# Sparse attention and routed experts on one core: a strided mask moved from TensorE to VectorE, one expert's weights loaded three steps later, and two warm-up products fewer

## The chip, the core and the metric

The kernel runs on one core of a Trainium2 chip. A core has five engines that each work through their own list of instructions in order and wait for one another through semaphores: TensorE (PE in the profile; its weight loads are PEld), VectorE (DVE), ScalarE (ACT), GpSimd (POOL) and SyncE (SP), which here issues most of the transfers. The transfers themselves are carried out by 16 DMA engines. The metric is the device time of one execution in microseconds.

## The reference

Eight batches of 576 tokens go through attention with 8 heads of 64, and then through a layer of eight experts of which each token uses one.

```python
# q, k, v: (B=8, H=8, S=576, D=64); stride = 32; scale = 1/8
rel = pos[:, None] - pos[None, :]
mask_local   = (rel >= 0) & (rel < 32)
mask_strided = (rel >= 0) & (pos[None, :] % 32 == pos[:, None] % 32)
# heads 0..3 use mask_local, heads 4..7 mask_strided
attn = softmax(where(mask, scale * q @ k.T, -1e9)) @ v
x = attn.transpose(0, 2, 1, 3).reshape(B, S, 512)
logits = x @ w_gate                       # 8 experts
local_gate = sigmoid(x @ w_local)
for b, s in all tokens:
    fresh = argmax(logits[b, s])
    e = fresh if s == 0 or local_gate[b, s] < 0.5 else previous e
    out[b, s] = softmax(logits[b, s])[e] * (relu(x[b, s] @ w1[e]) @ w2[e])   # w1[e] 512x1024, w2[e] 1024x512
```

A token of a strided head sees only the tokens of its own residue class modulo 32, and of those the ones up to itself.

## The kernel before

**Steps.** The attention stage is one Python loop (L450) over 32 steps, with three more at its end. Step n handles one batch and one pair of heads, n = 4 × batch + pair. Pairs 0 and 1 of a batch are local heads, pairs 2 and 3 are strided heads. Each step has two units (L428), and a unit handles about half the tokens of both heads in one PSUM tile `sps`, of which there are two.

**Local units.** The tokens are cut into spans of 96 queries with the 128 keys that they can see. TensorE multiplies keys by queries (L264), ScalarE takes the exponential (L268), and VectorE multiplies it by a mask of ones and zeros, `maskL` (L275).

**Strided units.** The host has sorted the tokens by residue class. Seven classes of 18 tokens make a block of 126, and the last block has four classes, 72 tokens; a unit has two blocks, or two and the one of 72. Within a block only pairs of the same class in causal order count. Before it adds the scores, TensorE writes the mask into PSUM: an identity matrix times `maskS` (L258), which holds 0 for pairs that count and a value of −8e9 for the others. The scores are added to that (L264, which does not start a new sum there), and the exponential gives zero where the mask is. VectorE has no mask to apply then. The four such mask products of a step are 252 or 324 columns wide. `maskS` is built at the start of the kernel (L209 to L225) from `apart`.

**Order within a step.** A step issues, in this order: the loads of step n + 4 (L451, function `load`: a tile qk of queries and keys, L169, and once per batch and kind the values, vl or vs, L173); a piece of the weights of expert 0 (L454); the scores and masks of its two units; the store of a finished batch half to device memory (`store_x`, L314 and L320, when the pair of step n − 2 is odd); the transposes `turn_x` of step n − 2 (L330); the products with the values (L288) and the normalisation on VectorE (L301, L302) of step n − 1. After these come the gate's logits and the router's work, which `also` spreads over the steps from 19 on. Each engine keeps the order in which its instructions are issued.

**Queues.** All loads of the attention stage and the pieces of the weights are issued by SP, and so are the stores of batches 1 to 7; the stores of batch 0 are issued by POOL. The store of local heads is two transfers, that of strided heads ten. SP's transfers share eight completion semaphores in turn, so that an issue waits for the transfer that was issued eight before it. There are five qk tiles, so that the load of step n + 4 waits until the scores of step n − 1 are done.

**Expert 0.** The weights of the first expert (4 MB) are loaded in eight pieces of 512 KB, one a step, at steps 5 to 12 (L454, L455; transfers at L724 and L727). From step 10 on VectorE takes sums of these pieces (`moe.W[0].sums`, L456, L732; 128x512 operations), two a step at the end of a step (L483). They are needed by the expert stage only, which begins at about 158 us and runs to the end.

**Warm-up.** While the first loads are on their way, TensorE multiplies a tile of zeros ten times (`busy(WARM)`, L186, 128x512 products into `vps`).

Of the kernel before, what the change touches and what calls it, by code (L numbers as in the profile page):

```python
# [8 lines left out]
F32 = mybir.dt.float32  # L9
# [3 lines left out]
Alu = mybir.AluOpType  # L13
# [6 lines left out]
B, H, S, DH = 8, 8, 576, 64  # L20
# [19 lines left out]
GK, GL = PL * GC, PL * GR  # L40
# [15 lines left out]

TRUST = 1e12

WARM = 10

FILL = 4

TWINS = {b: b - 1 for b in range(1, B - 1, 2) if b % RB}

# [20 lines left out]
def across(ap, shape):  # L85

    return ap.rearrange("a (o b) -> a o b", o=1).to_broadcast(shape)
# [60 lines left out]
def attention(ctx, tc, qkl, qks, vl, vs, wg, xd, ident, router, moe):  # L148

    nc = tc.nc  # L150
    sums, probs, codes = router.sums, router.probs, router.codes
    consts = ctx.enter_context(tc.tile_pool(name="consts", bufs=1))
# [11 lines left out]
    def load(b, pair):  # L164
        local = pair < PAIRS // 2
        src = qkl if local else qks
        t = inp.tile([P, qkl.shape[-1]], F32, name="qk")
        st["qk", b, pair] = t
        nc.sync.dma_start(out=t[:, 0:src.shape[-1]], in_=src[b, pair % 2])  # L169
        if pair % 2 == (b == 0 and local):  # L170
            shape = [LK, LT, 4, V1] if local else [GK, GT, 4, V1]
            t = vals.tile(shape, F32, name="vl" if local else "vs")
            nc.sync.dma_start(out=t, in_=(vl if local else vs)[b])  # L173
            st["v", b, local] = t
# [6 lines left out]
    def busy(n):  # L181
        for _ in range(n):
            ps = psV.tile([P, 512], F32, name="vps")
            nc.tensor.matmul(ps, lhsT=warm[:, 0:P], rhs=warm, start=True, stop=True)  # L184

    busy(WARM)  # L186

# [21 lines left out]
    maskS = consts.tile([GK, 2 * GK + GL], BF16, name="maskS")  # L209
# [3 lines left out]
    for n, c in blocks:  # L213

        i, div = consts.tile([GK, 1], I32, name=f"row{n}"), consts.tile([GK, 1], F32, name=f"div{n}")
# [7 lines left out]
    n = GK  # L223
    nc.vector.tensor_copy(maskS[:, 0:2 * n].rearrange("p (a x) -> p a x", a=2), across(apart[n], [n, 2, n]))
    nc.vector.tensor_copy(maskS[:, 2 * n:], apart[GL])  # L225
    fold = consts.tile([P, 32], F32, name="fold")
    ci = consts.tile([P, E], I32, name="ci")
    down = consts.tile([P, E], F32, name="down")
    pi = consts.tile([P, CH], I32, name="pi")
    pos8 = consts.tile([P, CH], F32, name="pos8")  # L230
    start = consts.tile([P, CH], F32, name="start")

    def more_constants():

        nc.vector.tensor_reduce(fold, ident.rearrange("p (k x) -> p x k", k=DK), axis=AX.X, op=Alu.add)


        nc.gpsimd.iota(ci, pattern=[[-1, E]], base=E, channel_multiplier=0)
        nc.vector.tensor_copy(down, ci)
        nc.gpsimd.iota(pi, pattern=[[E * P, CH]], base=E, channel_multiplier=E)  # L240
        nc.vector.tensor_copy(pos8, pi)
        nc.vector.tensor_scalar(start, pos8, float(E), None, Alu.is_equal)

    def spans(u):

        if u.local:
            return [(3 * u.g + i, LQ, i * LQ) for i in range(3)]
        return [(j, GK if j < GT - 1 else GL, i * GK) for i, j in enumerate(range(2 * u.g, 2 + 3 * u.g))]

    def scores(u):  # L250
        t = st["qk", u.b, u.pair]
        kb, width = (LK, LQ) if u.local else (GK, GK)
        ps = psS.tile([P, 2, 512], F32, name="sps")
        sp = spans(u)
        n = sp[-1][2] + sp[-1][1]
        if not u.local:
            for h in range(2):
                nc.tensor.matmul(ps[0:GK, h, 0:n], lhsT=identb[0:GK, 0:GK],  # L258
                                 rhs=maskS[:, 0:n], start=True, stop=False, skip_group_check=True)
        for j, w, c in sp:  # L260
            m = kb if u.local else w
            for h in range(2):
                r = slice(h * DH, (h + 1) * DH)
                nc.tensor.matmul(ps[0:m, h, c:c + w], lhsT=t[r, S + j * width:S + j * width + m],  # L264
                                 rhs=t[r, j * width:j * width + w],
                                 start=(u.local and c == 0), stop=True, skip_group_check=True)
        e = work.tile([P, 2, 2 * GK + GL], F32, name="e")
        nc.scalar.activation(e[0:kb, :, 0:n], ps[0:kb, :, 0:n], Act.Exp, bias=0.0, scale=1.0 / DH ** 0.5)  # L268
        u.e = e

    def mask(u):
        if u.local:
            ev = u.e[:, :, 0:3 * LQ]
            m = maskL[:, 3 * u.g:3 * u.g + 3].rearrange("p a x -> p (a x)")
            nc.vector.tensor_tensor(ev, ev, m.rearrange("p (o x) -> p o x", o=1).to_broadcast([LK, 2, 3 * LQ]),  # L275
                                    op=Alu.mult)

    def values(u):
# [151 lines left out]
        u.n = n  # L430

    also = {n: [] for n in range(len(units) + 3)}
    also[1] = [more_constants]
    also[2] = [router.constants]
    n = PAIRS * RB + 3
# [4 lines left out]
    m = n  # L440
    rooms = (moe.spot[0].rearrange("p a x -> p (a x)")[:, 0:1024], moe.spot[1].rearrange("p a k x -> p (a k x)"),
             moe.spot[2].rearrange("p i a x -> p (i a x)"))
    early = router.table(0, bank, rooms)
# [6 lines left out]
    for n in range(len(units) + 3):  # L450
        if n < len(units):  # L451
            if n + ahead < len(order):
                load(*order[n + ahead])
            if 5 <= n < 13:  # L454
                moe.W[0].load(nc, moe.w1, moe.w2, 0, n - 5)  # L455
            if n == 10:  # L456
                steps = moe.W[0].sums(nc.vector)
            for u in units[n]:
                scores(u)
                mask(u)  # L460
        if 0 <= n - 2 < len(units) and order[n - 2][1] % 2 == 1:
            store_x(units[n - 2][1])
        if 0 <= n - 2 < len(units) and n != len(units):
            turn_x(*order[n - 2])
        if 0 <= n - 1 < len(units):
            for u in units[n - 1]:
                values(u)
                norm(u)
        if n == len(units):
            turn_x(*order[n - 2])  # L470
            moe.turn(moe.first, spare, 0)
        elif n == len(units) + 1:
            busy(FILL)
        for b in range(B):
            last = PAIRS * b + PAIRS - 1
            if n == last + 3 and b + 1 not in TWINS:
                gates(b)
            if n == last + 4 and b < B - 1 and b + 1 not in TWINS:
                for both in {TWINS.get(b, b), b}:
                    store_p(both)  # L480
            if n == last + 2:
                logits(b)
        for do in steps[:2]:  # L483
            do()
            steps.remove(do)
        if n == len(units) + 1:
            moe.turn(moe.first, bank, 1)
            busy(2)
            moe.row_sums(moe.first)
        for do in also[n]:  # L490
            do()
# [1056 lines left out]
```

## Time and profile before

| What | Value |
| --- | --- |
| Time, median of 3 runs | 677.26 us (677.22 to 678.85) |
| Profiled execution: its own time | 677.25 us |
| Profiled execution: span of the core | 675.5 us |
| TensorE busy | 661.2 us, 98% of the span |
| VectorE busy | 353.9 us, 52% |
| ScalarE busy | 195.4 us, 29% |
| Attention stage | about 0 to 158 us |
| Expert stage | about 158 us to the end |

The profile is of one execution. Its span goes from the first to the last instruction, and the execution took 1.75 us more than that. A row of groups or of the timeline names the line, the engine, the operation, the tile written and the tiles read, the shapes, and how often it ran. A bracket with an arrow names what the engine waited for just before. "SPq" is SP issuing a transfer. A line with "DMA" in a chain of waits is the time in which a transfer was under way and somebody waited for it. "PE sps L264" is TensorE at the score products, "PE vps L184" at the products of zeros.

### The profile page before, as it was taken

The page shows a single profiled execution, that of the slowest core. Times are in us where ns is not written, and L with a number is a line of the kernel's source. Part 1 is how long each engine was busy: PE and PEld are TensorE (multiplying, and loading weights), DVE is VectorE, ACT ScalarE, POOL GpSimd, SP SyncE. Part 2 cuts the span into 40 slices and gives each one's busy share as a digit, 9 for nine tenths or more (in the row PEclk, how much of TensorE's full clock was granted, in tenths as well). Part 3 has the DMA queues.
Part 4 walks back from the last instruction along what each step waited for, and adds up shares of the span by engine and source line. Part 5 has one row for each costly group of instructions (what it writes and reads, how often), then busy time and mean ns, then how long its engine had stood idle before and what let it go on. Part 6 is the DMA issues. An engine that isn't in the chain of part 4 may idle for free.

```text
span 675.5 us, 14755 instructions
## 1 busy us (share of the span) xinstructions
PE 661.2 (98%) x6019; PEld 569.9 (84%) x6020; DVE 353.9 (52%) x783; ACT 195.4 (29%) x364; POOL 109.3 (16%) x132
## 2 busy tenths in 40 slices
PE   9999999999999999999999999999999999999995
PEld 6888888888999999599979999996799899699594
DVE  5658876956884447126523664651256546522122
ACT  3545445453312221321222222121222132221320
POOL 3401010122022023012011202302011112121001
PEclk9999999999999999999999999999999999999999
DMA  9998787875311081171145217101712622011001
GB/s 324 391 353 276 267 282 258 280 239 195 124 65 49 18 312 58 28 283 49 36 155 172 65 52 265 64 21 40 262 41 65 220 93 73 34 43 58 17 9 37
DMA packets 36435, 95.85 MB, mean 142 GB/s; under 512 B 4594, under 2 KB 12658, under 8 KB 36262
## 3 DMA queue, kind: packets, MB, share of 16 engines
q1 hardware_dynamic: 28438, 72.59, 30.7%
q0 software_dynamic: 7296, 21.19, 9.8%
q8 instruction: 67, 1.10, 0.7%
q14 instruction: 106, 0.87, 0.4%
q10 hardware_dynamic: 528, 0.10, 0.1%
HBM read 74.69 MB, written 19.69 MB: 140 GB/s over the span
## 4 chain that ended last, share of the span: by engine, by line
PE 94%; DVE 2%; DMA 1%; issue 1%; ACT 0%; SPq 0%; POOL 0%; DVEq 0%; POOLq 0%; ACTq 0%
PE lps L835 30%; PE mps L871 29%; PE sps L264 6%; PE vps L288 6%; PE lps L926 4%; PE mps L937 4%; PE tps L330 3%; PE xps L778 2%; PE mps L967 2%; PE lps L947 2%; PE sps L258 2%; DMA qk<-in_qks_dram 1%; PE tps L354 1%; PE vps L184 1%; PE tps L382 1%
## 5 line engine op out<-in xcount | busy, mean ns | idle before, releaser
L791 POOL DMA_INDIRECT out_dram<-y,tab x40 | 45.8, 1146 | 351.0 <-DVE y L823 246.6
L835 PE MATMUL lps<-tt,ws 128*128 128x128 f32 x768 | 91.5, 275 | 0.0
L835 PEld LDWEIGHTS lps<-tt,ws 128*128 128x128 f32 x768 | 88.5, 192 | 0.2
L871 PE MATMUL mps<-wt,k 128*128 128x256 f32 x384 | 85.7, 380 | 0.0
L871 PEld LDWEIGHTS mps<-wt,k 128*128 128x128 f32 x384 | 72.8, 190 | 9.9
L835 PE MATMUL lps<-xt,w1t 128*128 128x128 f32 x512 | 63.1, 276 | 3.0 <-ACT y L973 1.9
L835 PEld LDWEIGHTS lps<-xt,w1t 128*128 128x128 f32 x512 | 60.4, 192 | 6.5 <-ACT y L973 3.7
L823 DVE TENSOR_TENSOR h<-lps,u 128x512 f32<-128x512 f32 x48 | 33.2, 691 | 58.6 <-PE lps L835 58.5
L871 PE MATMUL mps<-w2t,h 128*128 128x256 f32 x256 | 60.5, 379 | 0.0
L268 ACT ACTIVATE e<-sps 128x576 f32<-128x576 f32 (+1 forms) x64 | 41.7, 651 | 54.7 <-PE sps L264 53.5
L765 POOL DMA_INDIRECT x<-xd,gi x40 | 40.2, 1005 | 82.4 <-PE lps L835 24.0
L871 PEld LDWEIGHTS mps<-w2t,h 128*128 128x128 f32 x256 | 47.4, 190 | 5.8
L264 PE MATMUL sps<-qk 64*128 64x96 f32 (+2 forms) x704 | 50.9, 282 | 0.8 <-DMA qk<-in_qks_dram 0.8
L822 ACT ACTIVATE h<-h 128x512 f32<-128x512 f32 x48 | 30.2, 630 | 70.1 <-DVE h L823 69.0
L264 PEld LDWEIGHTS sps<-qk 64*128 64x128 f32 (+2 forms) x704 | 42.9, 185 | 9.0 <-issue 6.5
L822 ACT ACTIVATE h<-lps 128x512 f32<-128x512 f32 (+1 forms) x28 | 15.6, 563 | 81.8 <-PE lps L835 62.6
L823 DVE TENSOR_TENSOR u<-lps,p 128x512 f32<-128x512 f32 x16 | 11.1, 691 | 51.8 <-PE lps L835 31.4
L771 ACT ACTIVATE x<-x 128x512 f32<-128x512 f32 (+1 forms) x40 | 27.1, 717 | 32.7 <-DMA x<-xd,gi 21.3
L779 ACT COPY xt<-xps 128x512 f32<-128x512 f32 (+1 forms) x38 | 20.3, 565 | 51.4 <-PE xps L778 51.4
L835 PE MATMUL lps<-xt,ws 128*128 128x128 f32 x256 | 31.3, 275 | 0.0
L835 PE MATMUL lps<-tt,w1t 128*128 128x128 f32 x256 | 31.3, 275 | 0.0
L871 PE MATMUL mps<-w2t,k 128*128 128x256 f32 x128 | 30.4, 380 | 0.0
(238 smaller groups left out, 952.2 us busy)
## 6 DMA issues: line engine op xcount, KB each, us to landing
w1t<-in_w_dram SPq DMA_DIRECT2D x7, 2048.0 KB
w2t<-in_w_dram SPq DMA_DIRECT2D x7, 2048.0 KB
qk<-in_qkl_dram SPq DMA_DIRECT2D x16, 592.0 KB
qk<-in_qks_dram SPq DMA_DIRECT2D x16, 576.0 KB
vl<-in_vf_dram SPq DMA_DIRECT2D x8, 780.0 KB
vs<-in_vg_dram SPq DMA_DIRECT2D x8, 639.8 KB
xd<-xl SPq DMA_DIRECT2D x14, 288.0 KB
xd<-xs SPq DMA_DIRECT2D x56, 63.0 KB
```

Source lines behind the costliest of these rows:

```text
L264: nc.tensor.matmul(ps[0:m, h, c:c + w], lhsT=t[r, S + j * width:S + j * width + m], rhs=t[r, j * width:j * width + w], start=(u.local and ...
L268: nc.scalar.activation(e[0:kb, :, 0:n], ps[0:kb, :, 0:n], Act.Exp, bias=0.0, scale=1.0 / DH ** 0.5)
L288: nc.tensor.matmul(ps[a * HALF:(a + 1) * HALF, h, i], lhsT=u.e[0:m, h, q0:q0 + HALF], rhs=vt[0:m, j, 2 * i2 + h], start=(i == 0 and h == 0 ...
L765: self.nc.gpsimd.indirect_dma_start(out=r.x[0:r.m, i], out_offset=None, in_=self.xd[0:r.rows], in_offset=bass.IndirectOffsetOnAxis(ap=r.gi ...
L771: self.nc.scalar.activation(r.x[0:r.m, i, 0:D], r.x[0:r.m, i, 0:D], Act.Copy, scale=r.gate[i][0:r.m])
L791: s = self.nc.gpsimd.indirect_dma_start(out=self.out, out_offset=bass.IndirectOffsetOnAxis(ap=r.si[i][0:r.m], axis=0), in_=y[0:r.m, i], in ...
L822: relu = lambda o, i: nc.scalar.activation(o, i, Act.Relu)
L823: add = lambda o, i, p: nc.vector.tensor_tensor(o, p, i, op=Alu.add)
L835: nc.tensor.matmul(ps[:, f], lhsT=m[:, kk, f * P:(f + 1) * P], rhs=v[:, kk], start=(start and f == 0 and kk == 0), stop=(kk == 1), skip_gr ...
L871: nc.tensor.matmul(ps[:, 0:256], lhsT=m[:, f], rhs=v[:, f], start=(start and f == 0), stop=(f == 3), skip_group_check=True)
L926: nc.tensor.matmul(ps[:, f], lhsT=w.w1[:, kk, c:c + P], rhs=r.xt[:, 0, kk], start=(f == 0 and kk == 0), stop=(kk == DK - 1), skip_group_ch ...
L937: nc.tensor.matmul(ps, lhsT=h[f // 4][:, f % 4], rhs=w.w2[:, f], start=(f == 0), stop=(f == FK - 1))
```

## The change

For the strided pairs of batches 0 and 1 (`MB = 2`) the mask is no longer written into PSUM by TensorE. VectorE multiplies the exponential by `near`, which is 1 where `maskS` is 0 and 0 elsewhere, as it does for local heads. `near` is computed once, at the end of step 0. In the block of 72 such a unit now computes all 126 rows of scores, and the mask sets what is too much to zero. To have rows enough there, queries and keys of strided heads change places in the tile that is loaded, on the host and in the kernel (`k0`, `q0`). Batches 2 to 7 keep the mask on TensorE.

The eight pieces of expert 0's weights are loaded at steps 8 to 15 instead of 5 to 12, and the sums begin at step 13 instead of 10. The warm-up has eight products instead of ten.

```diff
@@ -56,9 +56,11 @@
 
 TRUST = 1e12
 
-WARM = 10
+WARM = 8
 
 FILL = 4
+
+MB = 2
 
 TWINS = {b: b - 1 for b in range(1, B - 1, 2) if b % RB}
 
@@ -223,6 +225,7 @@
     n = GK
     nc.vector.tensor_copy(maskS[:, 0:2 * n].rearrange("p (a x) -> p a x", a=2), across(apart[n], [n, 2, n]))
     nc.vector.tensor_copy(maskS[:, 2 * n:], apart[GL])
+    near = consts.tile([GK, 2 * GK + GL], F32, name="near")
     fold = consts.tile([P, 32], F32, name="fold")
     ci = consts.tile([P, E], I32, name="ci")
     down = consts.tile([P, E], F32, name="down")
@@ -230,6 +233,9 @@
     pos8 = consts.tile([P, CH], F32, name="pos8")
     start = consts.tile([P, CH], F32, name="start")
 
+    def masks():
+        nc.vector.tensor_scalar(near, maskS, 0.0, None, Alu.is_equal)
+
     def more_constants():
 
         nc.vector.tensor_reduce(fold, ident.rearrange("p (k x) -> p x k", k=DK), axis=AX.X, op=Alu.add)
@@ -253,17 +259,20 @@
         ps = psS.tile([P, 2, 512], F32, name="sps")
         sp = spans(u)
         n = sp[-1][2] + sp[-1][1]
-        if not u.local:
+        early = u.b < MB
+        if not u.local and not early:
             for h in range(2):
                 nc.tensor.matmul(ps[0:GK, h, 0:n], lhsT=identb[0:GK, 0:GK],
                                  rhs=maskS[:, 0:n], start=True, stop=False, skip_group_check=True)
         for j, w, c in sp:
-            m = kb if u.local else w
+            m = kb if u.local or early else w
             for h in range(2):
                 r = slice(h * DH, (h + 1) * DH)
-                nc.tensor.matmul(ps[0:m, h, c:c + w], lhsT=t[r, S + j * width:S + j * width + m],
-                                 rhs=t[r, j * width:j * width + w],
-                                 start=(u.local and c == 0), stop=True, skip_group_check=True)
+                k0, q0 = (S, 0) if u.local else (0, S)
+
+                nc.tensor.matmul(ps[0:m, h, c:c + w], lhsT=t[r, k0 + j * width:k0 + j * width + m],
+                                 rhs=t[r, q0 + j * width:q0 + j * width + w],
+                                 start=((u.local or early) and c == 0), stop=True, skip_group_check=True)
         e = work.tile([P, 2, 2 * GK + GL], F32, name="e")
         nc.scalar.activation(e[0:kb, :, 0:n], ps[0:kb, :, 0:n], Act.Exp, bias=0.0, scale=1.0 / DH ** 0.5)
         u.e = e
@@ -273,6 +282,11 @@
             ev = u.e[:, :, 0:3 * LQ]
             m = maskL[:, 3 * u.g:3 * u.g + 3].rearrange("p a x -> p (a x)")
             nc.vector.tensor_tensor(ev, ev, m.rearrange("p (o x) -> p o x", o=1).to_broadcast([LK, 2, 3 * LQ]),
+                                    op=Alu.mult)
+        elif u.b < MB:
+            n = 2 * GK + (GL if u.g else 0)
+            ev = u.e[0:GK, :, 0:n]
+            nc.vector.tensor_tensor(ev, ev, near[:, 0:n].rearrange("p (o x) -> p o x", o=1).to_broadcast([GK, 2, n]),
                                     op=Alu.mult)
 
     def values(u):
@@ -430,6 +444,7 @@
         u.n = n
 
     also = {n: [] for n in range(len(units) + 3)}
+    also[0] = [masks]
     also[1] = [more_constants]
     also[2] = [router.constants]
     n = PAIRS * RB + 3
@@ -451,9 +466,9 @@
         if n < len(units):
             if n + ahead < len(order):
                 load(*order[n + ahead])
-            if 5 <= n < 13:
-                moe.W[0].load(nc, moe.w1, moe.w2, 0, n - 5)
-            if n == 10:
+            if 8 <= n < 16:
+                moe.W[0].load(nc, moe.w1, moe.w2, 0, n - 8)
+            if n == 13:
                 steps = moe.W[0].sums(nc.vector)
             for u in units[n]:
                 scores(u)
@@ -1526,7 +1541,7 @@
         return np.concatenate([a[:, :, :, c:c + GC].reshape(B, h2, -1, a.shape[4]) for c in range(0, STRIDE, GC)], 2)
 
     qkl = np.concatenate([heads(i["q"][:, :h2]), np.zeros((B, 2, P, STRIDE), np.float32), heads(i["k"][:, :h2])], 3)
-    qks = np.concatenate([heads(classes(i["q"][:, h2:])), heads(classes(i["k"][:, h2:]))], 3)
+    qks = np.concatenate([heads(classes(i["k"][:, h2:])), heads(classes(i["q"][:, h2:]))], 3)
     vf = np.stack([vp[:, :, t * LQ:t * LQ + LK] for t in range(LT)], 2).transpose(0, 3, 2, 1, 4)
     vg = np.concatenate([classes(v[:, h2:]), np.zeros((B, h2, GK * GT - S, V1), np.float32)], 2)
     vg = vg.reshape(B, h2, GT, GK, V1).transpose(0, 3, 2, 1, 4)
```

## The prediction, made before the change was run

> **What bounds the kernel now.** I read the page first: the span, the busy shares, and the row of DMA tenths.
>
> ```profile
> span 675.5 us, 14755 instructions
> PE 661.2 (98%) x6019; PEld 569.9 (84%) x6020; DVE 353.9 (52%) x783; ACT 195.4 (29%) x364; POOL 109.3 (16%) x132
> DMA  9998787875311081171145217101712622011001
> ```
>
> TensorE is busy 98% of the span, so whatever it no longer has to do ought to come off the end. But each digit of the DMA row is 16.9 us, and the first nine (152 us) are 7 to 9: in the attention stage, where the whole change lies, the transfers are nearly as full as TensorE. Both can set the time there, so I looked at stretches of that stage (columns: length, then PE, PEld, DVE, ACT and POOL busy with counts, PE clock, DMA share, GB/s).
>
> ```profile
> 8.07:24.50 16.43, 16.43 (x307) 14.25 (x307) 12.60 (x44) 7.81 (x13) 1.96 (x3) 1.00 1.02 362
> 24.50:37.30 12.80, 12.80 (x232) 10.12 (x229) 4.82 (x13) 7.27 (x14) 5.28 (x10) 1.00 1.03 382
> ```
>
> PE has no gap, and the DMA share is at 1: they run level. Which one is ahead shows in the chain of waits between 92 and 112 us.
>
> ```profile
> 95.58 0.38 SPq L169
> 95.97 0.05 issue
> 96.02 1.75 SPq L173
> 97.77 0.05 issue
> 97.82 0.02 SPq L169
> 97.83 0.03 issue
> 97.86 8.40 DMA qk<-in_qks_dram
> 106.26 0.04 issue
> 106.31 0.71 PE sps L264 x8
> ```
>
> Step 23 (batch 5, last pair) does not start when TensorE comes to it; it starts when its qk tile lands at 106.26. PE waited 0.78 us there. That load stands on SP's queue behind ten stores, as SP's timeline shows:
>
> ```profile
> 43.78 11.23 SPq L320 DMA_DIRECT2D xd<-xs  x10
> 55.11 0.40 SPq L169 DMA_DIRECT2D qk<-in_qks_dram  x1
> ...
> 64.59 12.73 SPq L320 DMA_DIRECT2D xd<-xs  x10
> 77.44 0.39 SPq L169 DMA_DIRECT2D qk<-in_qks_dram  x1
> ...
> 82.27 13.19 SPq L320 DMA_DIRECT2D xd<-xs  x10
> 95.56 0.40 SPq L169 DMA_DIRECT2D qk<-in_qks_dram  x1
> ```
>
> Once per batch SP goes through four steps' loads and ten stores, and only then issues the next strided load. The ten stores take 11 to 13 us although one issue is 0.75 us, and SP's waits there (43 to 116 us) end almost all on an earlier transfer ("SPq L320 <- DMA ..."), none over 1.2 us on PE. So from 43 us on SP goes at the speed at which transfers complete, and not at that of TensorE. This is the point on which my forecast rests.
>
> [...]two stretches at share 1.02 and 1.03 move 362 and 382 GB/s, and the stores and loads of one queue hold each other up. [...] The local mask (L275), a product, has 754 ns. [...] The ten warm products take 4.45 us, 0.44 each; score products in step 0 are 0.213 us apart until about 7.35 us and 0.107 after it. So the rise is seen, some 6 us after the first product.
>
> **Part 1, mask to VectorE (batches 0 and 1).** Four strided pairs, each with two units of two mask products.
>
> ```profile
> 15.77 0.43 PE L258 MATMUL sps<-maskS,identb 126*126 126x252 bf16 x2
> 16.13 0.71 PE L264 MATMUL sps<-qk 64*126 64x126 f32 x8
> 16.77 0.49 PE L258 MATMUL sps<-maskS,identb 126*126 126x324 bf16 x2
> 17.19 0.83 PE L264 MATMUL sps<-qk 64*126 64x126 f32 x12
> ```
>
> From start to start, 15.77 to 16.13 and 16.77 to 17.19, is 0.36 + 0.42, and some 0.1 goes at the change of weights: 0.87 us a pair, 3.48 us over steps 2, 3, 6 and 7. The score products stay as many; the last one's free size of 72 is kept while its 72 rows become 126, which adds nothing on PE. ACT reads the same 504 or 648 elements.
>
> On VectorE come 8 products of 504 and 648 elements: [...]back to back about 1.43 us a pair, as for a local pair. Each stands ahead of the norm of the step before, whose xs the transposes need; SP's stores wait for that norm too. There is one new compare (`near`), bounded by the rows of L220 between 0.2 and 0.65 us; I take 0.35. Cover: VectorE is busy 12.60 of 16.43 us up to 24.50, so it has 3.83 idle, and about 0.35 + 2 × 1.43 = 3.2 comes in. That does fit, but the transposes of step 5 wait for the norm that ends at 24.50, and by then TensorE can be only about 1.2 us ahead. From 24.50 to 37.30 VectorE has 8 us idle and takes 2.9, so steps 6 and 7 are won whole: 1.2 + 2 × 0.87 gives a lead of 2.9 at step 8 at the most. I take 2.4 (2 to 3.5), as the next norms follow closely.
>
> **Part 2, eight warm products.**
>
> ```profile
> 1.36 4.45 PE L184 MATMUL vps<-warm 128*128 128x512 bf16 x10 [1.36 <-DVE warm L179]
> ```
>
> Two fewer: 2 × 0.43 = 0.85 us. The first qk lands at 4.71 and the scores start at 5.74, so they can start about 4.9. If the clock rises at the same moment, 0.85 us more of score products run at half the rate, and about 0.4 is left; if it rises later, nothing or a loss of up to 0.9. This lies inside the 1.2 us above, so it adds nothing to step 8. Tiles 0 to 3 land up to 1.2 us before use, which bounds the early lead as well.
>
> **Part 3, expert 0's eight pieces of 512 KB from steps 5–12 to steps 8–15.** These are eight issues on SP. Nobody needs the tiles before 158 us, so what counts is the place in SP's queue. Ahead of the stores of step 9 stood five pieces and now stand two: three transfers less. The first five pieces land 1.53, 1.26, 1.25, 1.28 and 1.26 us apart, 1.32 on average: about 3.9 us earlier, so the load at 55.11 is issued near 51.2. The cycle after it has four pieces for three, the next two for none. What a piece costs there comes from the intervals between the strided loads at 55.11, 77.44, 95.56, 115.13 and 133.09: 22.33 with three pieces, and 18.12, 19.57 and 17.96 with none (18.55 on average), so (22.33 − 18.55)/3 = 1.26. Three more: 3.8. The load issued at 77.44 then comes near 51.2 + 22.33 + 1.3 = 74.8, and the one at 95.56 at 74.8 + 18.12 + 2.5 = 95.4. **By step 22 the eight pieces have all passed in both kernels, and the loads of steps 22 and 23 are where they were**, within 0.2 us.
>
> The sums of the weight pieces (16 VectorE operations of about 0.65 us, two a step) go from steps 10–17 to 13–20. They stand ahead of the next step's masks and norms. The latest piece, w2's last, should land about 86 us; its sum waits in step 18 or later, and if the piece is late, masks and norms behind it are late. Two sums (1.3 us) fall ahead of the scan of step 20 (L565, 1.33 us), whose next matmul is a step away. ACT and POOL keep their orders.
>
> **The sum.** TensorE is 2.4 us ahead at step 8 (starting at 34.9 instead of 37.3) and keeps that while loads are early. They then land at 81.67 for step 18 (used 81.71), 86.66 for 19 (87.47), 89.74 for 20 (91.96), 93.12 for 21 (95.49), 99.75 for 22 (100.71) and 106.26 for 23. Steps 18 to 21 have their loads 2.6 us earlier, so they hold the lead; at 22 the margin is 0.96, at 23 it is nothing. The lead of 2.4 turns into waits for qk in these two steps, which rise from 0.78 to about 3.2 us. After step 23 all is as before. The profiled execution took 677.25 (675.5 and 1.75 around it), the median of the runs is 677.26; I take 677.25 − 0.2, so 677.0.
>
> **The rivals.** *The lead survives (faster).* The issue at 96.02 took 1.75 us where its like take 0.41 (55.56, 77.88), and qk(23) is issued 1.35 later for it; the load of 99.30 took 2.07. They lie beside VectorE's scans (96.31 and 101.29). If in the new order these do not meet, the loads from 23 on come 1.4 to 2.4 earlier. Against it: the scan keeps its step, and the SP issue its time. Full lead: 677.25 − 2.4 = 674.85; half of it, 676.
>
> *Pieces cost more in their new place (slower).* One piece, issued at 56.95 between strided and local loads, landed 2.62 us after the one ahead. If three of the displaced pieces cost 2.6 instead of 1.26, the loads of 22 and 23 land 4 us later less what the ring absorbs; with two of them, 2.6. The place is step 23: it costs time as soon as qk(23) lands later than 106.26, all of the delay, and is over the bound from 2 us on. About 679.5. The intervals of 18 to 22 us, even with three pieces, speak against it.
>
> *VectorE becomes the bound* in steps 3 to 5: a lead of 0 to 1 at step 8; the time is 677.2, since the same load sets step 23. *The warm-up is too short*: half-rate products to about 10 us, up to 1 us lost early; caught by the same wait, 677.2.
>
> **How the numbers follow.** 0.3% is 2.0 us, about what a measurement of this kernel can tell from no change. Lead eaten by the load of step 23, 0.38, with the two last rivals, which end there, 0.10, and a lead kept in part, 0.09: same. Lead kept beyond 2.0 us: 0.25, or a little better still through loads that come early all along: 0.04. Pieces dearer: 0.14 beyond the bound. So faster 0.29, same 0.57, slower 0.14. The range goes from the full lead with a little over, 674.6, to the dearer pieces, 679.4.
>
> **What would show it.** Step 8's first score product near 34.9; SP's strided loads near 51.2, 74.8 and 95.4; qk(23) landing near 106; the wait of PE at L264 for qk in steps 22 and 23 at about 3 us in sum. If qk(23) lands before 104.5, or the wait does not grow while step 8 is early, the forecast is wrong to the fast side; if it lands after 108.3, to the slow one.

## The result, and the profile after

| What | Before | After |
| --- | --- | --- |
| Time, median of 5 runs | 678.85 us (677.22 to 679.21) | 686.64 us (685.90 to 690.05) |
| Ratio, 95% interval | | 1.0138 (1.0115 to 1.0161) |
| Profiled execution | 677.25 us | 690.05 us (its slowest) |

The medians lie 7.8 us apart, and the ratio says 1.4%, some 9 us; repeated further down, it was 1.0%. The forecast was no change. The profiled execution of the changed kernel is the slowest of its five, 12.8 us above that of the kernel before; a second profile of the same kernel, of an execution of 684.04 us, is used further down.

The top of the page of the changed kernel:

```profile
span 688.2 us, 14730 instructions
PE 662.6 (96%) x6002; PEld 572.4 (83%) x6002; DVE 360.0 (52%) x792; ACT 195.3 (28%) x364; POOL 109.1 (16%) x132
DMA  9989778866211170171217118121532442011001
```

TensorE is busy 1.4 us longer than before although 18 products are gone, and its share fell from 98% to 96%. So it stood still, and some products ran slower. First the place that the forecast was about. SP's timeline of the changed kernel, the stores and the strided load behind them:

```profile
39.31 11.26 SPq L334 DMA_DIRECT2D xd<-xs  x10
50.68 0.40 SPq L171 DMA_DIRECT2D qk<-in_qks_dram  x1
...
62.22 12.11 SPq L334 DMA_DIRECT2D xd<-xs  x10
74.45 0.58 SPq L171 DMA_DIRECT2D qk<-in_qks_dram  x1
...
82.52 12.87 SPq L334 DMA_DIRECT2D xd<-xs  x10
95.49 0.40 SPq L171 DMA_DIRECT2D qk<-in_qks_dram  x1
```

The forecast was 51.2, 74.8 and 95.4; before, they were issued at 55.11, 77.44 and 95.56. The lead that these loads gain on SP is given back by the third, as worked out. Step by step, the first exponential of the step on ScalarE, which follows the scores closely, shows what TensorE makes of it:

| Step | Before, us | After, us | Lead | Landing of its qk, before and after |
| --- | --- | --- | --- | --- |
| 1 | 9.05 | 7.76 | 1.29 | 6.54, 6.64 |
| 8 | 38.31 | 34.98 | 3.34 | 29.11, 28.50 |
| 19 | 88.22 | 84.96 | 3.26 | 86.66, 83.87 |
| 20 | 92.99 | 90.67 | 2.32 | 89.74, 89.61 |
| 21 | 96.50 | 94.20 | 2.31 | 93.12, 93.04 |
| 22 | 101.93 | 101.00 | 0.94 | 99.75, 100.20 |
| 23 | 107.06 | 107.26 | −0.20 | 106.26, 105.41 |
| 31 | 146.58 | 146.78 | −0.21 | 141.42, 141.75 |

The attention stage ends 0.2 us later than before. All of this execution's loss comes after it. Compared operation by operation on VectorE, the lag is 0.20 us at 160 us, 1.44 at 234, and 11.34 at 249. This is TensorE's timeline there, of the changed kernel (start, length, engine, line; in brackets the idle time and what ended it):

```profile
231.72 0.19 PE L715 MATMUL xps<-fine 128*1 128x1 f32 x2
233.10 5.42 PE L886 MATMUL mps<-wt,k 128*128 128x256 f32 x24 [1.19 <-DVE flag L718]
238.35 1.04 PE L793 MATMUL xps<-ident,x 128*128 128x128 f32 x8
239.23 1.89 PE L886 MATMUL mps<-w2t,k 128*128 128x256 f32 x8
244.45 3.62 PE L850 MATMUL lps<-xt,w1t 128*128 128x128 f32 x16 [3.33 <-issue]
250.91 5.47 PE L850 MATMUL lps<-tt,ws 128*128 128x128 f32 x32 [2.83 <-issue]
256.21 1.95 PE L850 MATMUL lps<-xt,w1t 128*128 128x128 f32 x16
```

And of the kernel before:

```profile
231.51 0.19 PE L700 MATMUL xps<-fine 128*1 128x1 f32 x2
231.63 5.45 PE L871 MATMUL mps<-wt,k 128*128 128x256 f32 x24
236.91 1.04 PE L778 MATMUL xps<-ident,x 128*128 128x128 f32 x8
237.79 1.89 PE L871 MATMUL mps<-w2t,k 128*128 128x256 f32 x8
239.52 1.95 PE L835 MATMUL lps<-xt,w1t 128*128 128x128 f32 x16
241.30 3.74 PE L835 MATMUL lps<-tt,ws 128*128 128x128 f32 x32
```

The same products in the same order; after the change TensorE stands still for 1.19, 3.33 and 2.83 us, and twice "issue" is all that the profile has for a cause: no semaphore came late. ("DVE flag" in the first is a wrong trail: `flag` had been written at 232.4, 0.65 us before the products started, and they do not read it.) Two groups after the gaps take 3.62 and 5.47 us instead of 1.95 and 3.74. The stretches 237.9 to 244.4, 244.4 to 250.9 and 250.9 to 256.3 of the changed kernel say why (PE clock in the third column from the end):

```profile
237.90:244.40 6.50, 3.22 (x19) 2.54 (x17) 2.70 (x7) 1.07 (x2) 2.03 (x2) 1.00 1.01 336
244.40:250.90 6.50, 3.62 (x16) 3.46 (x16) 0.00 (x0) 0.58 (x1) 0.00 (x0) 0.74 1.00 348
250.90:256.30 5.40, 5.39 (x33) 5.39 (x34) 0.69 (x1) 0.00 (x0) 2.11 (x3) 0.68 0.51 157
```

After standing still TensorE has a mean clock of 0.74 and 0.68; within these stretches it is 0.50 from 244.45 to 247.75 and from 251.25 to 254.60, and 1.00 from 247.9 to 251.1. The gaps make 7.35 us and the slower groups (3.62 + 5.47) − (1.95 + 3.74) = 3.40: together 10.75 of the 11.14 us that the lag grows between 160 and 249 us.

What lies between these products is a jump. Each expert has seven versions of the end of its work (`tc.Switch`, one for each number of row tiles left); TensorE, ScalarE, VectorE and GpSimd jump to one and, at its end, back. Ahead of a jump a hint names the target. The jump at 229 us is the first, that of expert 1. TensorE's own jumps in 215 to 248 us, before and then after (the line of the instruction; PEldq, TensorE's sequencer, which works through its list of instructions; count; least/median/most ns; first and last start):

```profile
L1544 PEldq COMPARE_BRANCH  x2: 446/935/1424, 228.9 to 236.5; - x2
```

```profile
L1559 PEldq COMPARE_BRANCH  x2: 3501/4920/6340, 229.3 to 237.9; - x2
```

The jump into expert 1's version took 0.45 us and takes 3.50; the jump out of it took 1.42 and takes 6.34. The sequencer ran ahead of its engine: when the late jump began at 229.33, 27 weight loads and products issued before it had not started, and they kept TensorE busy until 231.91, so that 3.50 us of jump leave a gap of 1.19. The later jumps of this line take 0.30 to 0.40 us in the changed kernel. The trace also shows a DMA queue of the kind "instruction", which moves blocks of 16,384 bytes, from 14 to 211 us one for every 250 traced instructions of TensorE on average. Before the change such a block is fetched at 225.55, 42 traced instructions ahead of the jump at 228.94. After it the fetches are at 214.97, 242 instructions ahead of the jump, and at 230.00, 0.7 us after the jump began.

So theory 1, my guess from these distances, is: the change took 36 weight loads and products off TensorE and added three waits, 33 fewer in all; every later instruction moved by 33 places against these blocks; and the jump now comes when its target has not been fetched. What a block holds no trace shows. A second figure goes with the guess, over all the fourteen traces of this document: TensorE stood still 21 times for 0.7 us or more with "issue" as the only cause, and each time it went on 2.2 to 2.8 us after such a block had begun to be fetched (241.75 and 248.32 for the gaps above that ended at 244.45 and 250.91). The rivals are the waits for qk with the halved clock after them (0.50 from 101.1 to 104.4 us in the changed kernel) (2), the later weights (3) and the mask on VectorE itself (4).

### The profile page after: what moved, and what is told of

It reads as the page before. It is cut to its first block, busy times and chain, and to the rows that moved or that the text cites. A ratio compares the mean times of both kernels' runs of the same rounds, so it can differ in the third digit from the quotient of the medians.

```text
span 688.2 us, 14730 instructions
## 1 busy us (share of the span) xinstructions
PE 662.6 (96%) x6002; PEld 572.4 (83%) x6002; DVE 360.0 (52%) x792; ACT 195.3 (28%) x364; POOL 109.1 (16%) x132
## 4 chain that ended last, share of the span: by engine, by line
PE 57%; issue 1%; DVE 1%; DMA 1%; ACT 0%; POOL 0%; POOLq 0%; ACTq 0%
PE lps L850 22%; PE mps L886 21%; PE mps L952 4%; PE lps L941 3%; PE mps L982 2%; PE lps L962 2%; PE xps L793 2%; DMA x<-xd,gi 1%; PE lps L972 0%; DVE h L973 0%; ACT y L988 0%; POOL out_dram L806 0%; DVE wt L747 0%; DVE y L838 0%; ACT x L786 0%
## 5 line engine op out<-in xcount | busy, mean ns | idle before, releaser
L806 POOL DMA_INDIRECT out_dram<-y,tab x40 | 45.8, 1145 | 362.4 <-DVE y L838 257.9
L850 PE MATMUL lps<-tt,ws 128*128 128x128 f32 x768 | 93.4, 279 | 3.8 <-issue 3.8
L850 PEld LDWEIGHTS lps<-tt,ws 128*128 128x128 f32 x768 | 90.2, 195 | 4.3 <-issue 4.1
L850 PE MATMUL lps<-xt,w1t 128*128 128x128 f32 x512 | 64.7, 281 | 6.3 <-issue 4.5
L850 PEld LDWEIGHTS lps<-xt,w1t 128*128 128x128 f32 x512 | 61.9, 196 | 10.1 <-issue 6.1
L273 PE MATMUL sps<-qk 64*128 64x96 f32 (+3 forms) x704 | 50.0, 282 | 2.6 <-DMA qk<-in_qks_dram 2.3
L838 DVE TENSOR_TENSOR u<-lps,p 128x512 f32<-128x512 f32 x16 | 11.1, 691 | 59.6 <-PE lps L850 39.3
```

The source lines that it names most:

```text
L273: nc.tensor.matmul(ps[0:m, h, c:c + w], lhsT=t[r, k0 + j * width:k0 + j * width + m], rhs=t[r, q0 + j * width:q0 + j * width + w], start=( ...
L806: s = self.nc.gpsimd.indirect_dma_start(out=self.out, out_offset=bass.IndirectOffsetOnAxis(ap=r.si[i][0:r.m], axis=0), in_=y[0:r.m, i], in ...
L838: add = lambda o, i, p: nc.vector.tensor_tensor(o, p, i, op=Alu.add)
L850: nc.tensor.matmul(ps[:, f], lhsT=m[:, kk, f * P:(f + 1) * P], rhs=v[:, kk], start=(start and f == 0 and kk == 0), stop=(kk == 1), skip_gr ...
```

## The experiments

All ratios are to the kernel before on the same chip, with a 95% interval. "Count" is the number of TensorE instructions ahead of the jump against the kernel before: −33 in the changed kernel.

**The instructions put back, the time of the work kept.**

```diff
-    busy(WARM)            # 8 products of 512 columns
+    busy(26, 158)         # 26 products of 158 columns, count +3
```

(In all the edits shown, comments are added and lines left out; the second number of `busy` is the columns.)

> The changed kernel with its warm-up cut otherwise: 26 products of zeros with 158 columns in place of 8 with 512, the same columns in all, but 36 more TensorE instructions (18 weight loads, 18 products) ahead of everything. Theory 1, fetch: the loss of the change is the jump into expert 1's arm, which TensorE's queue takes 3.5 + 6.3 us for since its place among the instruction blocks of 16 KB has moved; the net count of TensorE instructions ahead of it is then +3 against the kernel before instead of -33, a block is fetched between the hint and the jump, the two jumps take under 2 us as before, and the time is 677 to 678 (ratio 0.998 to 1.002). Theory 2, the waits for qk in steps 22 and 23 and the halved clock after them cost the time: they stay, so 686. Theory 3, the later weights and sums: they stay, so 686.

679.2 us, ratio 1.0012 (0.9994 to 1.0030); profiled 678.07. The jumps, from 215 to 248 us:

```profile
L1559 PEldq COMPARE_BRANCH  x2: 451/898/1344, 230.0 to 237.5; - x2
```

The loss is gone, with the mask, the later weights and all other work as in the changed kernel. Waits for qk in steps 22 and 23 are there (0.55 and 1.21 us), so they do not cost the 9 us, nor do the later weights or the mask. The halved clock after such a wait did not come up in this profile, whose mean granted clock is 0.998; theory 2 falls on the place of the loss, since the attention stage of the changed kernel with its halved clock ends 0.2 us late and not 9. One side effect: 26 small products take longer than 8 large ones, the lead at step 8 is 0.85 us only, and the stage ends 1.0 us late.

**TensorE as after, the rest as before.** The changed kernel without `near` and without its products on VectorE, and with the weights at steps 5 to 12.

> TensorE as in the changed kernel, instruction for instruction (-33 against before), but the new mask products and the compare on VectorE are left out, so strided pairs of batches 0 and 1 are not masked, and the weights load at steps 5 to 12 as before. Theory 1, fetch: the jump is still late, 685 to 690 (ratio 1.012 to 1.018), whatever VectorE and SP do. Theory 3, later weights, or a fourth, VectorE's extra work: 677 or less.

673.72 us, ratio 0.9907 (0.9874 to 0.9940), which looks like a miss of theory 1. Its profile says otherwise:

```profile
L1558 PEldq COMPARE_BRANCH  x2: 3545/4856/6168, 228.4 to 237.1; - x2
```

The jumps are as late as in the changed kernel, and VectorE's lag behind the kernel before grows from 0.6 to 11.1 us between 234 and 249 us. The shorter time comes later: without its mask the attention has other values, other tokens go to other experts, and from the jump at 409 us on the kernel runs other versions (the next jump is at 426.7 us, in the changed kernel at 415.1). As a time this run shows nothing; up to 260 us its trace can be compared with the others.

**Only the weights moved**, in the kernel before (steps 8 to 15, sums from 13; count 0).

> The kernel before with only expert 0's weights loaded at steps 8 to 15 and summed from step 13; TensorE's instructions are those of before (count 0). Theory 1, fetch: no change, 677 to 678, since the load of step 23 lands where it did. Theory 3, later weights: a loss of most of the 9 us, 685 or more.

677.78 us, ratio 0.9995 (0.9982 to 1.0008). The jumps take 0.45 and 1.92 us. SP issues the strided loads at 50.76, 76.08 and 96.47. Theory 3 falls by itself. Of the forecast of the SP cycle (51.2, 74.8 and 95.4) the first holds here within half a microsecond, the others come 1.1 to 1.3 later.

**Only the mask moved** (ten warm products, weights at steps 5 to 12; count −29).

> The changed kernel with ten warm products of 512 and the weights at steps 5 to 12 again: only the mask is moved. Count of TensorE instructions -29 against before. In the trace of before the jump came 42 instructions after a fetched block began, so here it should come about 13 after it: theory 1, fetch, expects a block fetched just ahead of the jump, so a jump that takes 1 to 3 us where it took 0.45, and 677 to 682; with theories 2 and 3 (waits for qk, later weights) 677, since the weights are where they were; if the mask itself costs, 686.

685.94 us, ratio 1.0126 (1.0102 to 1.0149); profiled 684.08. Here the expectation of theory 1 was off: the jump is not late by a little, it takes the full 3.50 us, and the second 1.89. I had counted that a block would be fetched 13 instructions ahead; none was, the next fetch began 1.0 us after the jump. The leads, taken as in the table above, say one thing more: with the weights at steps 5 to 12 the lead of 2.85 us at step 8 is lost in steps 17 and 18 (0.38 left), in the changed kernel in steps 20 to 23. In these two profiles the later weights moved the loss and did not remove it; the stage ends about where it did (here 0.06 us earlier at step 31).

**Where the edge lies.** The changed kernel with `busy(18, 228)`, count −13.

> The changed kernel with 18 warm products of 228 columns: 20 more TensorE instructions than it has, a count of -13 against before. It looks for the edge between -29 (late jump) and 0 (early). Theory 1: one or the other, not something between: 677 to 679 with a jump of 0.5 us if the block is fetched just before the jump, 684 to 687 with a jump of 3.5 us if not; TensorE's queue runs some ten to thirty instructions ahead of its products, so late is a little likelier. A theory by which the loss grows with the number of instructions left out expects about -13/33 of 9 us, 681.

681.0 us, ratio 1.0023 (1.0006 to 1.0040); profiled 680.36. The jump takes 0.456 us, with a fetch 28 instructions ahead of it: early, against my guess. So it is one or the other, and the edge is between −29 and −13. Most of what it takes longer is the attention stage's, 2.15 us by 160 us, of 3.1 in the profiled execution: qk of step 22 landed at 101.96 and TensorE was 1.97 us late at step 23.

**The same place by way of 222 more instructions**, in the kernel before. At 250 traced instructions from one block to the next, 222 more is by estimate the place of 28 fewer.

```diff
-    busy(WARM)            # 10 products of 512 columns
+    busy(121, 42)         # count +222
```

> The kernel before, with nothing moved, but its warm-up cut into 121 products of 42 columns instead of 10 of 512: 222 more TensorE instructions. [...] Theory 1, the place in the block decides: the two jumps of expert 1 take 3.5 and 2 to 6 us on TensorE's queue as in the changed kernel, and the expert stage is 7 to 11 us longer; time 685 to 690, with up to 3 us more or less for the many small products at the start. Theory 5, fewer instructions or the moved mask as such are the cause, and not the place: the jumps take 0.45 and 1.4 us, 677 to 680.

700.55 us, ratio 1.0322 (1.0280 to 1.0363). From 235 to 256 us:

```profile
L1544 PEldq COMPARE_BRANCH  x2: 1425/2414/3402, 242.3 to 250.9; - x2
```

The jump into the version is late (3.40 us), in a kernel in which only the warm-up is changed, and its count upward. The small products cost 10.8 us at the start (the first mask of VectorE starts at 18.84 instead of 8.07), which I had put at 3 at the most: 0.125 us from one to the next, of which the load of each one's weights takes 0.10. The lag at 200 us is 13.4 us, at the end 21.8; so the expert stage is 8.4 us longer: 3.5 around this jump, 1.2 around a gap that ends with "issue" at 309 us, and 3.8 around another (1.96 us at 502 us, just past a jump, and a mean clock of 0.79 from 500 to 508).

**136 more instructions**, `busy(78, 66)`.

> As the last, with 78 products of 66 columns: 136 more TensorE instructions than before, which puts a block's boundary in the middle between the hint and the jump of expert 1. Theory 1, the place in the block: the jump takes 0.3 to 0.5 us and the time is 677 to 680, the small products included. Theory 6, any large change of the count (or the small products) costs: 685 or more, as with 222.

686.64 us, ratio 1.0098 (1.0059 to 1.0137), which is outside what I expected. More than half of the loss is again the small products: VectorE's lag is 6.1 us at its first mask, 9.6 at 149 us, and 10.7 in the end. What made the 3.5 us between is not known. The jump is early:

```profile
L1544 PEldq COMPARE_BRANCH  x2: 351/1007/1663, 238.6 to 246.1; - x2
```

Of two kernels with more instructions than before, one is late at this jump and one is not. So theory 5 falls, and of theory 6 the part that any large change of the count would do; its other part, that small products cost, came true in the time. Another jump of this kernel, at 339 us, takes 3.45 us, with 1.3 us lost around it, though its hint stands 409 instructions ahead.

**The changed kernel again.**

> The changed kernel once more, since the profile shown of it was of its slowest execution (690.05 us against a median of 686.64): 685 to 688. Theory 1 expects the jump of expert 1 at 3.4 to 3.6 us on TensorE's queue again, the second jump (end of the arm) anywhere between 1.4 and 6.5 us, and in that spread the difference between executions.

684.79 us, ratio 1.0103 (1.0066 to 1.0140). In its profile of 684.04 us the jumps take 3.58 and 1.53 us:

```profile
233.06 5.42 PE L886 MATMUL mps<-wt,k 128*128 128x256 f32 x24 [1.18 <-DVE flag L718]
238.31 1.04 PE L793 MATMUL xps<-ident,x 128*128 128x128 f32 x8
239.19 1.89 PE L886 MATMUL mps<-w2t,k 128*128 128x256 f32 x8
240.92 1.95 PE L850 MATMUL lps<-xt,w1t 128*128 128x128 f32 x16
245.22 5.44 PE L850 MATMUL lps<-tt,ws 128*128 128x128 f32 x32 [2.36 <-issue]
```

The gap of 3.33 us is missing here. In both profiles the first jump is late; the second is very late in one only, and most of the difference between these two executions is that. The sum again: gaps 1.18 + 2.36, slower clock 5.44 − 3.74 = 1.70, together 5.24 of the 5.45 us that the lag grows between 160 and 249 us; in both executions about 1 more comes near 300 us, at another gap that ends with "issue" (0.99 and 0.71 us).

This profile also corrects the account of the attention stage. At step 8 TensorE is 3.37 us ahead again, but at step 10 it is 0.15 us behind, before any load of steps 20 to 23 matters. From 37.10 to 38.76 us it stood still in the midst of a group of 40 products, with "issue" as the cause and no jump near; a block had begun to be fetched at 36.19. From 38.76 to 45.8 its mean clock was 0.76, by estimate 1.7 us lost (0.24 of 7.04). So TensorE stood still with "issue" as the cause in a straight run of instructions too, and went on 2.57 us after a block had begun to be fetched; this execution lost its lead there.

**The hint earlier.** In the changed kernel the reading of `pick` and the hint go 120 instructions ahead.

```diff
-        places += [[lambda: next(arms)]]
+        places += [[lambda: next(arms)], [lambda: chosen.append(choose(1))]]
```

> The changed kernel with one thing moved: the reading of pick and the hint for expert 1's jump (choose) stand in the output of the pair before, some 70 weight loads and products earlier on TensorE. All counts stay, the offset of -33 too. From hint to jump it is then about 280 instructions instead of 210[...]. Theory 1, fetch: the jump takes 0.3 to 0.5 us, the loss goes, 677 to 678 (ratio 0.998 to 1.002) as the attention stage alone gives. If the jump is late for another reason (the load of the weights of expert 2, the count of instructions as such): 3.5 us and 686, as before the move.

686.81 us, ratio 1.0127 (1.0094 to 1.0159), and the jump takes 3.47 us:

```profile
L1561 PEldq COMPARE_BRANCH  x2: 1849/2660/3472, 230.9 to 239.5; - x2
```

A miss of the mechanism as I had it. The hint is now 330 traced instructions ahead, more than the 250 from one block to the next, a block was fetched between hint and jump (at 217.28 us, 224 instructions ahead), and the jump was late all the same. Why, no run shows. What the fourteen profiles show of this jump, sorted by the distance from the last fetch:

| Last fetch ahead of the jump, instructions | Kernels | Jump, us |
| --- | --- | --- |
| 28 to 44 | counts −13, −12, 0, 0, +3, +5 | 0.35 to 0.46 |
| 172 | +136 | 0.35 |
| 224 to 231 | early hint (−33 and −31), −29 | 3.47 to 3.55 |
| 240 to 242 | −33 three times, +222 | 3.40 to 3.58 |

The order of the table follows from the counts. In the kernel before a fetch began 42 instructions ahead of the jump; 42 plus the count, less 250 where it is more, is by estimate where that fetch would stand. It gives 29 to 47 for the first row and 178 for the second, close to what was measured, and 9 to 14 for every kernel with a late jump: there the fetch had not begun when the jump came. This describes this jump alone. In the kernel before, the jump at 573.8 us comes 230 instructions after the last fetch and takes 0.33 us.

**Where the lead goes, first try.** The run with 26 warm products, with the weights at steps 22 to 29 and sums from step 27.

> The kernel of the run with 26 warm products of 158 columns (mask moved, TensorE count +5), with expert 0's eight pieces loaded at steps 22 to 29 and summed from step 27 on. It asks where TensorE's lead of about 3 us at step 8 goes. Theory A, as the prediction has it: the lead is eaten in steps 22 and 23 by the loads that stand behind the eight pieces on SP; with the pieces later those loads come up to 8 x 1.26 = 10 us earlier, PE waits for no qk tile in steps 19 to 25, and the stage ends some 3 us earlier: 674 to 675 (ratio 0.994 to 0.996). Theory B, the lead is lost elsewhere (VectorE's masks, the clock): 677 to 678 although the tile of step 23 lands before 103 us. Theory C, the pieces only move the wait to steps 26 to 31: waits for qk there, 676 to 677.

679.88 us, ratio 1.0011 (0.9994 to 1.0029); profiled 678.22. Between theories A and B: no wait for qk is left in steps 19 to 25. The lead of 1.93 us at step 8 falls to 0.98 by step 22, is 1.84 at step 23, where the kernel before waits, and still 1.83 at step 29. In step 30 it is gone, for VectorE; the waits of PE from 128 to 143 us:

```profile
PE tps L344 <- DVE got L673: 1.8, 1, 1.8
```

VectorE's queue holds the sums of the weights ahead of the copy of `got` that PE waits for.

**Second try**, with the early hint and sums three a step from step 31.

> The same early hint, and expert 0's pieces at steps 22 to 29 with their sums from step 31 on, three a step, the rest after the stage. In the run with the pieces at 22 to 29 TensorE kept its lead up to step 29 and lost it in step 30, where VectorE's sums (steps 27 to 34) held up the copy of got that PE waited 1.8 us for. Theory A: with the full warm start TensorE is 3.3 us ahead at step 8, keeps 2.5 to 3.3 us through step 31, and 674 to 675 comes out (ratio 0.993 to 0.996). Theory B, VectorE is full from step 28 on whatever order its work has, or the sums come too late for the first products of expert 0: the lead is lost in steps 30 to 34 or at the first ws, 677 to 680.

686.83 us, ratio 1.0113 (1.0080 to 1.0147). The jump is late (3.55 us), since the earlier hint does not help. The lead was only 0.2 us at step 8 in the profiled execution: TensorE had waited 2.22 us for the qk of step 3, which landed at 16.29 instead of 14.30, and its next 20 score products took 2.41 us, where the 20 of step 2 took 1.32. At step 31 it was 0.98; in the first steps of the experts 2.2 us are lost to a wait for VectorE (`cum`). Nothing is settled by it, but that sums put off to the end are in the way there.

**A version for both causes.** The changed kernel with count −12, w1's pieces early and w2's late, each with its sums where VectorE has room.

```diff
-    busy(WARM)
+    busy(18, 228)
-            if 8 <= n < 16:                       # pieces, one a step
-            if n == 13:                           # all sums, two a step
+            if 12 <= n < 16 or 24 <= n < 28:      # w1's four, w2's four
+            if n == 18: ...                       # sums of w1, two a step
+            if n == 31: ...                       # sums of w2, two a step
```

> A version meant to beat both: the changed kernel with 18 warm products of 228 columns (count -12 against before; with -13 the jump of expert 1 was early), the four pieces of w1 at steps 12 to 15 with their sums at 18 to 21, the four of w2 at steps 24 to 27 with theirs at 31 to 34. Theory A: only the pieces ahead of the loads of steps 22 and 23 eat the lead; four fewer are 4 x 1.26 = 5 us, more than the lead of 2.7 us that this warm-up gave, and the sums now stand where VectorE has room, so that 2 to 2.7 us are left at step 31: 675 to 676 (ratio 0.995 to 0.998). Theory B: VectorE's sums late in the stage, or the loads of steps 26 to 31 behind the pieces of w2, take it back: waits for qk or on DVE after step 28, 677 to 679. The jump should take 0.5 us either way; if a place of -12 is late after all, 684 to 687.

675.83 us, ratio 0.9962 (0.9946 to 0.9978), profiled 673.70. It beats both kernels: its median is 2.1 us below that of the kernel before. In the profiled execution TensorE is 3.68 us ahead at step 8 and 4.00 at step 31; qk of step 23 lands at 99.41 instead of 106.26, and the jump is early:

```profile
L1561 PEldq COMPARE_BRANCH  x2: 456/910/1364, 224.9 to 232.5; - x2
```

## Why the prediction was wrong

**The mask on VectorE.** The lead at step 8 was forecast as 2.4 us (2 to 3.5) and is 3.34. The direction holds, and the cover on VectorE was there. The scores of step 3, with their masks, took TensorE 2.18 us before (15.77 to 17.95) and without them 1.26 (14.49 to 15.75): 0.92 less, 0.87 forecast. From the first to the third product of 72 columns it was 0.06 us in both kernels, with 72 rows and with 126. The eight new products on VectorE took 0.66 to 0.84 us, two of them back to back 1.41 to 1.57 (1.43 forecast), the compare 0.32 (0.35). But 1.29 us of the lead stood at step 1, before any mask had moved, and that is largely the chance of the start: the kernel with only the weights moved, whose TensorE runs the same instructions as before, is 0.94 us ahead at step 1. Its clock rose earlier: between 5.4 and 7.4 us 29 of its products were traced, 17 in the kernel before. From step 1 to step 8 seven of the nine profiles with the mask on VectorE, among them both of the changed kernel, gained 1.9 to 2.5 us, in line with the 2.4 forecast; the other two had stops in between (the 2.22 us wait for the qk of step 3 in one, two stops with "issue" of 0.44 and 0.77 us in the other). What the shorter warm-up is worth, put at 0.4, can't be told from this.

**The weights on SP.** In the profile of the changed kernel right within half a microsecond: three pieces less gave 4.4 us (3.9 forecast), and the cycles after it gave it back. The kernel with this edit alone shows no change in time, with the second and third load up to 1.3 us later than forecast.

**The lead eaten by the loads of steps 22 and 23.** Right in where the stage ends, +0.2 us in both profiles of the changed kernel, and right in part on the way there. In the first profile the lead goes in steps 20 to 23. The forecast had the loads of steps 18 to 21 land 2.6 us earlier; those of 18 and 19 did (3.3 and 2.8), those of 20 and 21 only 0.13 and 0.08, so that 0.94 us went at step 20 already. The waits for qk are smaller than the 3.2 us forecast, 1.77 at step 22 and none at step 23, because a slower clock after the first took its share:

```profile
98.00:100.20 2.20, 0.47 (x10) 0.19 (x2) 2.09 (x6) 1.41 (x4) 0.00 (x0) 1.00 0.73 188
100.20:105.90 5.70, 5.66 (x76) 4.61 (x76) 1.84 (x3) 1.94 (x3) 0.00 (x0) 0.70 0.97 292
```

In the second profile the lead was lost at steps 9 and 10 to the stop at 37.10 us and the slower clock after it, so that the forecast end was reached there by another way. That a lead can live when pieces are out of the way is shown by the version for both causes, in one profile: it is still 4.00 us at step 31.

**The step that failed is the last sentence of the sum, "After step 23 all is as before".** It rests on the instructions after step 23 being the same ones. They are, but they stand 33 places further ahead against the fetched blocks: the jump at 229 us comes 242 traced instructions after the start of the last fetch instead of 42, and needs 3.5 us instead of 0.45. With the jump out of the version, the gaps and the slower clock after them, that cost 11.14 us in the first profile of the changed kernel and 5.45 in the second. I had counted 18 products removed as time and never as places in a program. The sum had no such term, and none of the rivals did: the slower case that I had, dearer pieces on SP with step 23 as its place, did not happen (qk of step 23 landed 0.85 us earlier). So the range ended at 679.4. The profile of before had what was needed to ask: a queue of kind "instruction" in its page's part on DMA queues, and in its trace two of TensorE's 16 jumps of this line with 1.4 and 1.9 us where the others took 0.3 to 0.45.

What stays open is what makes a fetch come in time, and whether the hint has a part in it. The edge between −29 and −13, and the distances in the table, are what was measured. The jump out of the version took 6.2 and 6.3 us in two of the late profiles and 1.1 to 1.9 in the other five. In those five a third block had begun to be fetched 0.5 to 1.2 us ahead of it (at 236.86 in the second profile of the changed kernel), in the two none had, and the next fetch began 3.6 to 3.8 us after the jump did; why was not found.

## What to carry to other kernels

Where a program jumps, count the instructions that a change adds or removes on each engine, and compare the jumps' own durations in the trace; if idle time ends with "issue", look there first. A few small products ahead of the jump help to tell a fault of place from a fault of work, since they move the place and leave the work behind them as it is; look at the jump and not at the time alone, for they cost time themselves (121 of 42 columns put off VectorE's first mask by 10.8 us). Take more than one profile before a lost lead is put down to one cause. And a lead on the engine that bounds is only worth what the next supply allows: move the transfers that stand ahead of it in its queue in the same edit, and put the work that hangs on them where its engine has room.

## What the hardware showed that I had not expected

- The jump on TensorE into expert 1's version took 0.35 to 0.46 us in seven profiles and 3.4 to 3.6 us in the other seven, by its distance from the last fetch (28 to 44 and 172 traced instructions in the first seven, 224 to 242 in the others). The loss around the late one was 3.5 to 11.7 us. In the changed kernel 3.40 of its 10.75 us are slower products after the gaps, with a mean clock of 0.74 and 0.68 in stretches of 6.5 and 5.4 us.
- Every stop of TensorE of 0.7 us or more that ended with "issue", 21 in fourteen traces, ended 2.2 to 2.8 us after a block of 16,384 bytes had begun to be fetched. Three of them, of 0.77 to 1.66 us, stood in the attention stage, far from any jump.
- A low clock followed short gaps, sometimes. In the changed kernel TensorE was busy 0.47 of the 2.20 us from 98.0 to 100.2, and had a mean clock of 0.70 in the 5.7 us after it, with 0.50 from 101.1 to 104.4. But after a stop of 2.38 us that ended at 258.20, in the kernel with 222 more instructions, the mean clock stayed at 1.00.
- Products of 42 and 66 columns at the start of the kernel came 0.125 and 0.134 us apart: 121 of 42 put off VectorE's first mask by 10.8 us against ten products of 512, 78 of 66 by 6.1. Each has its own load of 128 columns of weights, of 0.10 us.
